# VectorE's outer products of batch 0 in one place, the key-value sums ahead of the denominators, q's second half turned between them; block 10's w_out product whole

## The chip, the cores and the metric

The kernel runs on one core of a Trainium2 chip. The metric is the device time of one execution in microseconds (us). Five engines matter here: TensorE (PE in the profile, its weight loads PEld), VectorE (DVE), ScalarE (ACT), GpSimd (POOL), and SyncE (SP), whose queue issues nearly all of the DMAs. Each engine works through its own instructions in order and waits on semaphores for the others.

## The reference

Two stages, the first feeding the second:

```python
# q, k, v: (4 batches, 4 heads, 1088 tokens, 32); S1, S2: (8, 32)
phi(x)  = outer(S1 x, S2 x)                      # 64 features a token
kv, z   = sum_s phi(k)_s v_s, sum_s phi(k)_s      # per batch and head
attn    = (phi(q) kv) / (phi(q) z + 1e-6)
x       = attn as (4352 tokens, 128)
out     = (sigmoid(x @ w_gate) * (x @ w_val)) @ w_out    # d_ff 1536
```

S1, S2 and the three weights arrive as 64-bit floats, and the kernel makes 32-bit floats of them itself.

## The kernel before

**The steady part.** The tokens are cut into nine chunks `ci` (eight of 512, one of 256). For each chunk and each of the twelve blocks j of 128 columns of d_ff, one *wave* (`w1`, L541) multiplies the chunk's attention result `xT` by block j of w_gate and of w_val into a PSUM tile `wave`; ScalarE makes the sigmoid `sg` (L564), VectorE the product `g` (L599), and TensorE multiplies `g` by block j of w_out. `slot` (L625) writes the order out by hand: in each slot the `g` of the wave before, the w_out products that have fallen due (list `todo`), then the next wave. Chunk 0 uses `w2` (L418), due two waves later; later chunks use an arrangement with fewer multiplications (`w2_a`, `w2_b`, L381), and the last one `w2_end`. In chunk 0 the waves use the whole array (128x128 weights); from chunk 1 on each wave is cut into two halves of 64 columns of the array that run side by side. In `w2`, blocks 0 to 9 are whole (`d = slice(0, P)`, L424), blocks 10 and 11 in two such halves. Block 10's product stands behind chunk 0's last wave and ahead of `kps(1)`, the first product of batch 1.

The attention work of batches 1 to 3 is put between waves (`plan`, L1353). Batch 0's can't be: no wave can start before its first 256 tokens are in `xT`. So the kernel has a *head*, the code from L1147 to L1249, which is what the change touches most.

**The head.** In the order in which the program issues it:

1. q, k, v and the weights are loaded (L282 to L293). SP's DMAs, in order: S, q's first half (8 of 17 pairs of rows), block 0 of w_gate and w_val, v, block 1 of both, w_out's first two blocks (`load_w_out(0)`, L289), q's second half (L290), then the other weights.
2. VectorE turns k and q's first half (`turn_k`, `turn_q(0, 0)`). `kps` (L683) gives S k for all tokens, `ab` (L784) S q for the first 512 tokens.
3. `gram` (L710) gives the sums z from products of S k with itself; GpSimd masks them (`gh`, L727), `spread_z` (L738, a matmul) spreads them, `mask_z` (L747, VectorE) makes the weights `zb` of the denominators.
4. `outer` (L769) forms phi(k) for nine blocks of tokens, `kp`. For each pair of heads pi, GpSimd does blocks 6 to 8 (L1206), VectorE blocks 0 to 4 (L1211) and, later, block 5 (L1220).
5. `mult00` and `mult10` (L819, VectorE) form phi(q), `qp`.
6. `kv0` (L894) multiplies v by phi(k): `kvz` in bank acc1, a matmul for each block and head. Each head has a strip of 32 columns of the array. Blocks 0 to 4 come before `mult00`, blocks 5 to 8 inside `rest`.
7. `dn(0, 0, rest)` (L1077): the denominators `dps` (L1083), then `rest` (L1218): block 5's outer products, the last `kv0`, the denominators turned (`dT`, L1094), 1e-6 added by ScalarE (`rc`), `kvz` copied (`kvd`, L934), steps of the weights, `ndt` (L959: kv turned, `ndps` and its copy `nd`); then the numerators `nps` (L1102).
8. `divide` (L1112): reciprocal, `rb` (the reciprocals spread, L1131), `between`, and the product `xT` (L1121), each for 256 tokens. `between` is `head1` (L1233): q's second half turned (`turn_q(0, 1)`), steps of the weights, and `qcomp` (L830: `cqps`, its ScalarE copy `cq`) with the DMAs that spread it.
9. `slot(None, 1)`: the first wave, whose first half needs 256 tokens of `xT` and block 0 of w_gate and w_val.

**Weights on the way.** `Short` (L129) makes 32-bit numbers in steps that go from engine to engine: `bounds` (ACT `cap`, then POOL `head` L141), `lower` (`tail`, ACT or DVE), `shift` (DVE L157), `total` (POOL L162), `sign` (ACT L168), `final` (DVE L171 into `w_sb`). Piece 0 is block 0 of w_gate and w_val, piece 1 block 1, piece 2 the first two blocks of w_out, piece 3 block 2 of all three, and so on.

Of the kernel before, what the change touches and what calls it, by code (L numbers as in the profile page):

```python
# [16 lines left out]
P = 128  # L17
# [3 lines left out]
def kernel(  # L21
# [12 lines left out]
    nc = tc.nc  # L34

    B, H, S, D = q.shape
# [4 lines left out]
    NJ = DFF // P  # L41
    assert DM == H * D == P and D == 32 and R == 8 and S % 32 == 0 and NTOK % 512 == 256

    T = S // 32

    NJK = 9
# [14 lines left out]
    psm = ctx.enter_context(tc.tile_pool(name="psm", bufs=2, space=bass.MemoryType.PSUM))  # L61
# [14 lines left out]
    T0 = 2 * q_chk[0][1]  # L76
# [116 lines left out]
    def load_w_in(j0, j1):  # L193
        cs = slice(j0 * P, j1 * P)
        n, jj = divmod(j0, 2)
        if wide and jj == 0:
            w_in[n] = raw.tile([P, 3, 2, P, 2], I32, tag="w_in", name="w_in")
        for i, src in enumerate((moe_w_gate, moe_w_val)):
            if wide:
                nc.sync.dma_start(  # L200
                    out=w_in[n][:, i, jj : jj + j1 - j0].rearrange("p j m w -> p (j m w)"),
                    in_=src[:, cs].bitcast(I32),
                )
            else:
                nc.sync.dma_start(
                    out=w_sb[:, i, j0:j1].rearrange("p j m -> p (j m)"), in_=src[:, cs]
                )

    def load_w_out(n):
        j0, j1 = 2 * n, 2 * n + 2  # L210
        cs = slice(j0 * P, j1 * P)
        src = moe_w_out[cs, :].bitcast(I32) if wide else moe_w_out[cs, :]
        nc.sync.dma_start(
            out=w_in[n][:, 2].rearrange("p j m w -> p j (m w)") if wide else w_sb[:, 2, j0:j1],
            in_=src.rearrange("(j p) m -> p j m", p=P),
        )
# [3 lines left out]
    def step(name, *parts, **how):  # L220
        for n in parts if wide else ():
            if n not in short:

                i = ((slice(0, 2), 0), (slice(0, 2), 1), (2, slice(0, 2)))[n] if n < 3 else (slice(0, 3), n - 1)
                pair, jj = (0, i[1]) if n < 3 else divmod(n - 1, 2)
                short[n] = Short(w_sb[:, i[0], i[1]], w_in[pair][:, i[0], jj])
            getattr(short[n], name)(**how)
# [15 lines left out]
    def load_rows(src, b, t, parts=((0, T, nc.sync),)):  # L243
        for t0, t1, eng in parts:
            eng.dma_start(
                out=t[:, t0:t1, :],
                in_=bass.AP(
                    tensor=src.tensor,
                    offset=src[b, 0].offset + t0 * D,
                    ap=[[T * D, P], [1, (t1 - t0) * D]],  # L250
                ),
            )

    v_sb = ld.tile([P, H, NJK, D], F32, tag="v", name="v")
    def load_v(b):
        base = v[b, 0].offset
        for g in range(4):
            j = g // 2
            nc.sync.dma_start(
                out=v_sb[32 * g : 32 * g + 32, :, j:],  # L260
                in_=bass.AP(
                    tensor=v.tensor,
                    offset=base + (KBASE[g] + j) * D,
                    ap=[[T * D, 32], [S * D, H], [1, (NJK - j) * D]],
                ),
            )

    k_t, q_t = {}, {}
# [17 lines left out]
    load_w_in(0, 1)  # L286
    load_v(0)
    load_w_in(1, 2)
    load_w_out(0)  # L289
    load_rows(q, 0, q_t[0], ((T0, T, nc.sync),))  # L290
    for n in range(1, NJ // 2):
        load_w_in(2 * n, 2 * n + 2)
        load_w_out(n)  # L293
# [124 lines left out]
    def w2(ci, j0, jn, g):  # L418
        if j0 == 0:
            moe["sum"] = ci  # L420
            moe["acc"] = pso.tile([P, TCH], F32, tag="acc0", name="moeout")
        for jj in range(jn):
            j = j0 + jj
            for d in (slice(0, P),) if j < NJ - 2 else (slice(0, 64), slice(64, P)):  # L424
                nc.tensor.matmul(  # L425
                    out=moe["acc"][d],
                    lhsT=w_sb[:, 2, j, d],
                    rhs=g[:, jj],
                    start=(j == 0),
                    stop=(j == NJ - 1),  # L430
                )
        if j0 + jn == NJ:
            o_sb = sbA.tile([P, TCH // 32, 32], F32, tag="o_sb", name="o_sb")
            nc.vector.transpose(out=o_sb.rearrange("p t d -> p (t d)"), in_=moe["acc"])
            moe["store"] = lambda: store(
                ci, lambda g4: o_sb[32 * g4 : 32 * g4 + 32], nc.scalar
            )
# [229 lines left out]
    def turn_q(b, n):  # L667
        if b >= B:
            return
        if n == 0:  # L670
            qT_of[b] = sbA.tile([P, TP, 2, 32], F32, tag="qT", name="qT", bufs=1)
        t0, tn = q_chk[n]
        nc.vector.transpose(
            out=qT_of[b][:, t0 : t0 + tn].rearrange("p t c s -> p (t c s)"),
            in_=q_t[b][:, 2 * t0 : 2 * (t0 + tn)].rearrange("p t d -> p (t d)"),
        )
# [92 lines left out]
    def outer(b, pi, j0=0, j1=NJK, eng=nc.vector):  # L769
        a0 = KAB[b][:, pi, j0:j1]  # L770
        ap = [list(a0.ap[0]), [2 * R, 2 * (j1 - j0)]]
        eng.tensor_tensor(  # L772
            out=KP[b][:, pi, j0:j1].rearrange("p j m (i l) -> p (j m) i l", i=R),
            in0=bass.AP(tensor=a0.tensor, offset=a0.offset, ap=ap + [[1, R], [0, R]]),
            in1=bass.AP(tensor=a0.tensor, offset=a0.offset + R, ap=ap + [[0, R], [1, R]]),
            op=MUL,
        )
# [113 lines left out]
        q0 = half(QP[b], n)  # L891
        nc.vector.tensor_tensor(out=q0, in0=q0, in1=half(BQ[b], n), op=MUL)  # L892

    def kv0(j_list):  # L894
        if 0 not in KVZ:
            KVZ[0] = pso.tile([P, TCH], F32, tag="acc1", name="kvz")
        for j in j_list:
            for h in range(H):
                nc.tensor.matmul(
                    out=KVZ[0][32 * h : 32 * h + 32, :F],  # L900
                    lhsT=v_sb[:, h, j, :],
                    rhs=KP[0][:, h // 2, j, h % 2, :],
                    start=(j == 1),
                    stop=(j == NJK - 1),
                    skip_group_check=True,
                )
# [23 lines left out]
    def kvd(b):  # L930
        KVD[b] = sbA.tile([P, 2, 2, F], F32, tag="kvd", name="kvd")
        k0 = KVZ[b][:, : 2 * F]
        n = 2 if b > 0 else 1
        nc.scalar.copy(  # L934
            out=KVD[b][:, :n],
            in_=bass.AP(
                tensor=k0.tensor, offset=k0.offset, ap=[list(k0.ap[0]), [F, n], [0, 2], [1, F]]
            ),
        )
# [19 lines left out]
    def ndt(b):  # L959
        if b == 0:  # L960
            t = pso.tile([P, TCH], F32, tag="acc1", name="ndps")
            ndps = t.rearrange("p (w x) -> p w x", w=2)
        else:
            ndps = ps2.tile([P, 2, 512], F32, tag="two", name="ndps")[:, 0].rearrange(
                "p (w x) -> p w x", w=2
            )
        if b == 0:
            nc.tensor.matmul(
                out=ndps[:, 0, :P],
                lhsT=KVD[b][:, 0].rearrange("p c f -> p (c f)"),  # L970
                rhs=ident,
                is_transpose=True,
                start=True,
                stop=True,
            )
        for c in range(2 if b else 0):
            nc.tensor.matmul(
                out=ndps[64 * c : 64 * c + 64, 0, :P],
                lhsT=KVD[b][:, 0, c],
                rhs=ident,  # L980
                start=True,
                stop=True,
            )
        ND[b] = sbA.tile([P, P], F32, tag="nd", name="nd")
        nc.scalar.copy(out=ND[b], in_=ndps[:, 0, :P])
# [222 lines left out]
    step("lower", 0, 1)  # L1208
    spread_z()
    for pi in range(2):  # L1210
        outer(0, pi, 0, 5)  # L1211
    kv0([1, 2, 3, 4, 0])
    mult00()
    mult10()
    mask_z()


    def rest(turn, rc, dT):  # L1218
        for pi in range(2):
            outer(0, pi, 5, NJK - 3)  # L1220
        kv0(range(5, NJK))
        turn()
        nt = rc.shape[1] - 1
        nc.scalar.activation(out=rc[:, :nt], in_=dT[:, :nt, :2], func=ACTF.Identity, bias=eps)
        kvd(0)
        step("shift", 0, 1)
        step("total", 0, 1)
        step("sign", 0, bank="acc0")
        ndt(0)

    divide = dn(0, 0, rest)

    def head1():  # L1233
        turn_q(0, 1)
        step("final", 0)
        step("sign", 1, bank="acc1")
        step("bounds", 2)
        step("lower", 2)
        step("bounds", 3)
        spread(0, (1,), qcomp(0, (1,), (psm, "wave")), nc.sync, nc.sync)  # L1240

    divide((0, 4), (4, 8), between=head1)
    step("final", 1)
    step("shift", 2, 3)
# [169 lines left out]
```

## Time and profile before

| | us |
|---|---|
| median of three runs | 290.53 (290.02 to 291.15) |
| the profiled execution | 289.88 |
| its span in the profile | 288.1 |
| TensorE busy | 282.3 (98%) |
| VectorE, GpSimd, ScalarE busy | 171.2, 159.7, 106.7 |
| first wave's first matmul | 14.44 |
| last matmul of the program issued | 284.6 |

Times in the profile count from the start of the span. What lies around the span in the profiled execution is 289.88 - 288.1 = 1.8 us. A line of the timeline gives the start, the length and the engine, then the line of the program, the operation, what it writes and reads, and how many instructions are put together in the line; for an x2 line the length is from the first one's start to the last one's end. VectorE's and ScalarE's instructions are pipelined, so that the next one often starts up to 0.1 us before the end of the one before. A 32-bit matmul stands as two instructions. The granted TensorE clock is at its full 1.0 in all slices.

### The profile page before, as it was taken

To read this page: it belongs to the slowest core of one execution; us is meant where nothing else is said; L and a number is where in the kernel's file an instruction comes from. 1 tells how busy PE (TensorE), PEld (TensorE's weight loads), DVE (VectorE), ACT (ScalarE), POOL (GpSimd) and SP (SyncE) were. 2 spreads that over 40 slices of the span, in tenths; PEclk is the share of its full clock that TensorE was granted. 3 is DMA by queue.
4 is the path that set the end of the run, shared out by engine and by line. 5 is a ranking of instruction groups with operands and counts; after the bars stand their busy time and mean duration, and the time that the engine had idled before them with its cause. 6 is when DMAs were issued, how large, how long until landed. Compare 5 with 4: busy or idle time off the path is not lost.

```text
span 288.1 us, 5789 instructions
## 1 busy us (share of the span) xinstructions
PE 282.3 (98%) x2262; PEld 134.4 (47%) x2262; DVE 171.2 (59%) x294; ACT 106.7 (37%) x215; POOL 159.7 (55%) x222
## 2 busy tenths in 40 slices
PE   8799999999999999999999999999999999999995
PEld 3454433354444444535444445444444444444685
DVE  6987788946748547668446485767245223522571
ACT  3788832222334322523244222532243224421341
POOL 2666682667466387383565496483564646555200
PEclk9999999999999999999999999999999999999999
DMA  7995441765700386451000673020001000020012
GB/s 215 338 371 122 111 156 43 167 143 126 207 2 2 77 192 155 108 164 29 1 0 12 159 181 102 2 30 9 0 3 23 14 2 0 4 35 1 0 19 40
DMA packets 28891, 24.24 MB, mean 84 GB/s; under 512 B 18560, under 2 KB 24064, under 8 KB 28864
## 3 DMA queue, kind: packets, MB, share of 16 engines
q1 hardware_dynamic: 25888, 22.10, 29.8%
q10 hardware_dynamic: 2976, 1.77, 2.1%
q8 instruction: 18, 0.29, 0.5%
q14 instruction: 9, 0.07, 0.1%
HBM read 20.60 MB, written 3.26 MB: 83 GB/s over the span
## 4 chain that ended last, share of the span: by engine, by line
PE 97%; ACT 1%; DVE 1%; issue 0%; POOL 0%
PE wave L556 61%; PE prod L381 22%; PE moeout L425 4%; PE moeout L451 2%; PE warm L301 2%; PE kvz L912 1%; PE nps L1271 1%; PE kps L693 1%; PE cqps L839 1%; PE nps L1102 0%; PE denj L1041 0%; PE dps L1083 0%; PE nps L1054 0%; ACT asb L810 0%; DVE qp L819 0%; PE aps L800 0%
## 5 line engine op out<-in xcount | busy, mean ns | idle before, releaser
L556 PE MATMUL wave<-xT,w_sb 128*64 128x512 f32 (+3 forms) x820 | 201.4, 565 | 0.0
L564 ACT ACTIVATE sg<-wave 128x512 f32<-128x512 f32 x102 | 60.9, 597 | 158.0 <-PE wave L556 152.0
L599 DVE TENSOR_TENSOR g<-wave,sg 128x512 f32<-128x512 f32 x96 | 66.0, 688 | 87.6 <-ACT sg L564 86.1
L371 POOL TENSOR_TENSOR tsum<-g,tsum 128x256 f32<-128x256 f32 x84 | 67.5, 804 | 71.0 <-DVE g L599 70.8
L556 PEld LDWEIGHTS wave<-xT,w_sb 128*64 128x64 f32 (+1 forms) x820 | 71.0, 140 | 72.5 <-issue 53.0
L371 POOL TENSOR_TENSOR tsum<-g 128x256 f32<-128x256 f32 x84 | 67.5, 804 | 22.3 <-DVE g L599 21.7
L381 PE MATMUL prod<-tsum,ws 128*64 128x256 f32 x252 | 68.4, 380 | 0.0
L381 PE MATMUL prod<-g,w_sb 128*64 128x256 f32 (+1 forms) x170 | 50.3, 378 | 0.0
L381 PEld LDWEIGHTS prod<-tsum,ws 128*64 128x64 f32 x252 | 34.0, 137 | 13.1 <-issue 9.7
L381 PEld LDWEIGHTS prod<-g,w_sb 128*64 128x64 f32 x170 | 23.0, 137 | 30.1 <-issue 25.8
L381 PE MATMUL prod<-tsum,w_sb 128*64 128x256 f32 x84 | 25.0, 380 | 0.0
L381 PE MATMUL prod<-g,ws 128*64 128x256 f32 x84 | 25.0, 379 | 0.0
L162 POOL TENSOR_TENSOR head<-head,tail 128x384 int32<-128x384 int32 (+1 forms) x13 | 13.2, 1022 | 4.3 <-DVE head L157 4.3
L381 PEld LDWEIGHTS prod<-g,ws 128*64 128x64 f32 x84 | 11.5, 137 | 5.7
L425 PE MATMUL moeout<-g,w_sb 128*128 128x512 f32 (+1 forms) x28 | 12.4, 600 | 0.0
L381 PEld LDWEIGHTS prod<-tsum,w_sb 128*64 128x64 f32 x84 | 11.3, 137 | 1.3 <-issue 1.0
L892 DVE TENSOR_TENSOR qp<-qp,bq 128x1152 f32<-128x1152 f32 (+1 forms) x7 | 10.5, 1502 | 0.3 <-DMA bq<-dq 0.3
L772 DVE TENSOR_TENSOR kp<-kab 128x1152 f32<-128x1152 f32 (+2 forms) x10 | 10.7, 1081 | 0.0
L592 DVE TENSOR_TENSOR g<-wave,sg 128x512 f32<-128x512 f32 x6 | 6.8, 1132 | 6.3 <-ACT sg L564 4.7
L496 DVE TENSOR_TENSOR res<-prod,other 128x256 f32<-128x256 f32 x14 | 5.9, 425 | 6.3 <-ACT other L487 4.8
L141 POOL TENSOR_SCALAR head<-cap 128x384 f32<-128x384 f32 (+1 forms) x13 | 6.3, 487 | 5.2 <-ACT cap L140 5.2
L152 ACT ACTIVATE tail<-w_in,two__157 128x384 f32<-128x384 uint32 (+1 forms) x12 | 7.2, 610 | 0.0
(130 smaller groups left out, 196.0 us busy)
## 6 DMA issues: line engine op xcount, KB each, us to landing
qp<-dq SPq DMA_DIRECT2D x7, 576.0 KB
bq<-dq SPq DMA_DIRECT2D x14, 288.0 KB
kq<-in_k_dram SPq DMA_DIRECT2D x3, 544.0 KB
kq<-in_q_dram SPq DMA_DIRECT2D x3, 544.0 KB
w_in<-in_moe_w_out_dram SPq DMA_DIRECT2D x6, 256.0 KB
w_in<-in_moe_w_gate_dram SPq DMA_DIRECT2D x5, 256.0 KB
w_in<-in_moe_w_val_dram SPq DMA_DIRECT2D x5, 256.0 KB
v<-in_v_dram SPq DMA_DIRECT2D x8, 144.0 KB
```

What stands on the lines that cost most here:

```text
L141: nc.gpsimd.tensor_scalar(out=self.head.bitcast(F32), in0=self.cap, scalar1=122880.0, scalar2=2.0**-15, op0=ALU.min, op1=ALU.max,)
L152: nc.scalar.activation(out=self.tail, in_=self.lo, func=ACTF.Identity, bias=two, scale=2.0**-51)
L162: nc.gpsimd.tensor_tensor(out=self.head, in0=self.head, in1=self.tail.bitcast(I32), op=ALU.add)
L371: nc.gpsimd.tensor_tensor(out=t[:, u], in0=in0, in1=in1, op=ALU.subtract)
L381: nc.tensor.matmul(out=out, lhsT=lhsT, rhs=rhs, start=start, stop=stop, skip_group_check=True)
L425: nc.tensor.matmul(out=moe["acc"][d], lhsT=w_sb[:, 2, j, d], rhs=g[:, jj], start=(j == 0), stop=(j == NJ - 1),)
L556: nc.tensor.matmul(out=wv[d, which, jj * tw + o : jj * tw + o + tp], lhsT=w_sb[:, which, j0 + jj, d], rhs=xT[:, t0 + o : t0 + o + tp], sta ...
L564: nc.scalar.activation(out=sg, in_=wv[:, 0], func=ACTF.Sigmoid)
L592: nc.vector.tensor_tensor(out=g.rearrange("p (j u s y) -> p j y u s", j=2, u=2, y=4), in0=wv[:, 1].rearrange("p (j y u s) -> p j y u s", j ...
L599: nc.vector.tensor_tensor(out=g, in0=wv[:, 1], in1=sg, op=MUL)
L772: eng.tensor_tensor(out=KP[b][:, pi, j0:j1].rearrange("p j m (i l) -> p (j m) i l", i=R), in0=bass.AP(tensor=a0.tensor, offset=a0.offset, ...
L892: nc.vector.tensor_tensor(out=q0, in0=q0, in1=half(BQ[b], n), op=MUL)
```

## The change

Five edits, all in the head but the second:

- q's second half is loaded ahead of w_out's first blocks.
- Block 10's w_out product of chunk 0 is whole; only block 11 stays in halves.
- VectorE's outer products cover blocks 0 to 5 in one instruction for each pair of heads. All of `kv0` stands ahead of `mult00` and of the denominators: blocks 1 to 5 and 0 for all heads, then GpSimd's blocks 6 to 8 for heads 0 and 1, then for heads 2 and 3.
- `turn_q(0, 1)` and `kvd(0)` come ahead of `dn`, and `ndt(0)` is the first thing in `rest`. So VectorE has q's second half between `zb` and `dT`, and ScalarE copies `kvd` and `nd` before `rc`.
- In `head1`, `spread` with `qcomp` comes ahead of `step("bounds", 3)`.

```diff
     load_w_in(1, 2)
+    load_rows(q, 0, q_t[0], ((T0, T, nc.sync),))
     load_w_out(0)
-    load_rows(q, 0, q_t[0], ((T0, T, nc.sync),))
...
-            for d in (slice(0, P),) if j < NJ - 2 else (slice(0, 64), slice(64, P)):
+            for d in (slice(0, P),) if j < NJ - 1 else (slice(0, 64), slice(64, P)):
...
-    def kv0(j_list):
+    def kv0(j_list, heads=range(H)):
...
         for j in j_list:
-            for h in range(H):
+            for h in heads:
...
     for pi in range(2):
-        outer(0, pi, 0, 5)
-    kv0([1, 2, 3, 4, 0])
+        outer(0, pi, 0, NJK - 3)
+    kv0([1, 2, 3, 4, 5, 0])
+    for pi in range(2):
+        kv0(range(NJK - 3, NJK), (2 * pi, 2 * pi + 1))
     mult00()
     mult10()
     mask_z()
+    turn_q(0, 1)
+    kvd(0)
 
 
     def rest(turn, rc, dT):
-        for pi in range(2):
-            outer(0, pi, 5, NJK - 3)
-        kv0(range(5, NJK))
+        ndt(0)
         turn()
         nt = rc.shape[1] - 1
         nc.scalar.activation(out=rc[:, :nt], in_=dT[:, :nt, :2], func=ACTF.Identity, bias=eps)
-        kvd(0)
         step("shift", 0, 1)
         step("total", 0, 1)
         step("sign", 0, bank="acc0")
-        ndt(0)
 
     divide = dn(0, 0, rest)
 
     def head1():
-        turn_q(0, 1)
         step("final", 0)
         step("sign", 1, bank="acc1")
         step("bounds", 2)
         step("lower", 2)
+        spread(0, (1,), qcomp(0, (1,), (psm, "wave")), nc.sync, nc.sync)
         step("bounds", 3)
-        spread(0, (1,), qcomp(0, (1,), (psm, "wave")), nc.sync, nc.sync)
```

## The prediction

> **What bounds the kernel.** I read first the share of busy time (TensorE 98%), then what TensorE itself waited for, over the whole program:
>
> ```profile
> PE dps L1083 <- DVE zb L762: 0.5, 1, 0.5
> PE ndps L968 <- ACT kvd L934: 0.5, 1, 0.5
> PE nps L1102 <- ACT nd L985: 0.4, 1, 0.4
> PE gram L739 <- POOL gh L727: 0.3, 1, 0.3
> ```
>
> Beside 0.8 us at the very start, that is all, and all of it lies in the head. From the first wave at 14.44 us on, TensorE has no idle time that the profile shows. So a change can pay in two ways only: an earlier first wave, or fewer TensorE microseconds behind it. The timelines by engine give the head, VectorE first:
>
> ```profile
> 7.49 1.52 DVE L772 TENSOR_TENSOR kp<-kab 128x640 f32<-128x640 f32 x2
> 8.99 1.29 DVE L819 TENSOR_TENSOR qp<-bps,asb 128x512 f32<-128x512 f32 x2
> ...
> 10.58 0.68 DVE L772 TENSOR_TENSOR kp<-kab 128x128 f32<-128x128 f32 x2
> 11.51 0.45 DVE L1094 STREAM_TRANSPOSE dT<-dps 128x256 f32<-128x256 f32 x1 [0.24 <-PE dps L1083]
> ...
> 12.62 0.45 DVE L1131 STREAM_TRANSPOSE rb<-rc 128x256 f32<-128x256 f32 x1
> 12.99 0.74 DVE L673 STREAM_TRANSPOSE qT<-kq 128x576 f32<-128x576 f32 x1
> 13.65 0.39 DVE L171 TENSOR_TENSOR w_sb<-square,head 128x256 f32<-128x256 f32 x1
> 13.96 0.42 DVE L1121 TENSOR_TENSOR xT<-nps,rb 128x256 f32<-128x256 f32 x1
> ```
>
> From `dT` to `xT` VectorE never waits 0.15 us; q's second half (`qT`) stands in the middle of that chain, and the product `xT` (done at 14.38) releases the first wave. GpSimd's and TensorE's lines:
>
> ```profile
> 8.65 0.46 POOL L727 TENSOR_TENSOR gh<-gs,e_m 128x32 f32<-128x32 f32 x1 [2.37 <-ACT gs L725]
> 9.07 1.65 POOL L772 TENSOR_TENSOR kp<-kab 128x384 f32<-128x384 f32 x2
> ```
>
> ```profile
> 9.50 0.77 PE L899 MATMUL kvz<-kp,v 128*32 128x64 f32 x40
> 10.81 0.64 PE L1083 MATMUL dps<-qp,zb 128*32 128x256 f32 x8 [0.55 <-DVE zb L762]
> ...
> 42.63 1.02 PE L425 MATMUL moeout<-g,w_sb 128*128 128x512 f32 x2
> 43.49 1.88 PE L556 MATMUL wave<-xT,w_sb 128*128 128x512 f32 x4
> 45.30 1.08 PE L425 MATMUL moeout<-g,w_sb 128*64 128x512 f32 x4
> 46.31 0.72 PE L693 MATMUL kps<-kT,sk 64*32 64x288 f32 x16
> ```
>
> The reader is to see that GpSimd's outer products run from 9.07 to 10.72, and that `dps` starts at 10.81, 0.14 behind `zb` (10.45 to 10.67).
>
> **Outer products in one place.** VectorE: the 640-element instruction takes 0.78 (7.49 to 8.27, the next starts at 8.19), the 128-element one 0.28. The slope is 0.50 / 512, so 768 elements cost 0.125 more each, 0.25 for two. The two small ones (0.68 behind `zb`) go. So `mult00` starts at 9.24, `zb` ends at 10.92.
>
> What else is late by that? `gh` is a small GpSimd instruction (128x32), yet it takes 0.46; a GpSimd copy of the same 128x32 at 6.05 takes 0.23. It ends at 9.11, 0.10 behind VectorE's second outer product (8.19 to 9.01). So I take it to be held by that one. The latter now ends at 9.26, `gh` at 9.36, and GpSimd's two outer products, right behind it, at 10.97 and not 10.72. The bounds for `gh`: not held at all, 0.00 later; held, 0.25 later. I take 0.25, by its own row. The Trainium skill weighs on the same side: "SBUF — State Buffer", section "Who interferes with whom", says that a VectorE instruction with two SBUF inputs and a GpSimd instruction that reads SBUF exclude each other for a whole instruction. That speaks against this change, which lengthens such an instruction just where GpSimd is waiting: by the rule the head's gain is the 0.05 below, without it the 0.32 of the first rival. The row alone leaves both readings open; the trace has no `gh` without a neighbour.
>
> **kv ahead of the denominators.** TensorE works in order, so `dps` now also waits for all of `kvz`, and the last twelve of its instructions (blocks 6 to 8 of heads 2 and 3) wait for GpSimd's second outer product: 10.97, plus 0.05 to the first matmul (VectorE's small product ended at 11.27, the weight load behind it came at 11.32). They use two strips of columns, six on each. The 40 at 9.50 use four strips, ten on each, and start within 0.77 - 0.22 (the last one's length) = 0.55, so 0.056 a step. Six steps: 0.34. `dps` starts at 11.36 instead of 10.81: +0.55. (By `zb` alone it would be 11.07.) Bounds of a step: 0.056, and 0.11, a weight load's length, if nothing overlaps on a strip. I take the first, which is measured.
>
> `kvd` and `ndt` come off the path: `kvz` is done at 11.57, `kvd` at 11.9, `ndps` behind `dps` at 12.3, `nd` at 12.6, the numerators end at 13.3 instead of 13.86. That gain has no taker: `xT` waits for `rb` and its place on VectorE.
>
> **q's second half moved.** On VectorE it stands between `zb` and `dT`: 10.84 to 11.58, while `dT` can't start before 12.06 (11.51 + 0.55). Free, with 0.48 to spare. Its data must be there by 10.84. SP has eight DMAs under way, and the one issued at 11.07 was released by q's second half, the one at 10.30 by w_out's first blocks (SP's waits name them). Exchanged, q lands near 10.3 and w_out near 11.05; the latter is first used at 13.5. On SP's queue nothing else changes place but these two (0.44 and 0.45 to issue). `qcomp`'s matmuls now end at 13.9 instead of 14.47.
>
> From `dT` on: before, `dT` 11.51, `rb` 12.62, `qT`, weights 13.65, `xT` 13.96. After: `dT` 12.06, `rb` 13.17, then the weights of block 0 at once (13.54) if GpSimd's `total` is there. `shift` starts 0.37 behind `dT`, `total` 0.40 behind that and lasts 0.73 (12.28 to 13.01 before): 13.56, plus 0.04. So weights 13.60, `xT` +0.31 = 13.91, first wave at 14.39: 0.05 earlier. In sum, 0.66 of `qT` and wait gone, 0.55 later `dps`, 0.06 of wait for GpSimd.
>
> Behind it the first wave's second matmul stood 0.32 behind the first instead of the later 0.22, beside `cqps`, which ended at 14.47; that 0.10 goes as well. But the first w_out product waits for VectorE's `g`, before at 17.15 to 17.83 with the product at 17.99. Its predecessors (`cap` of block 2, now behind the copy `cq` on ScalarE, GpSimd's `head` and `total`, the weights) come out within 0.05 of where they were, so I count 0.05 and not 0.15. Head: **-0.05**.
>
> **Block 10 whole.** A whole product costs 0.86 (42.63 to 43.49), a wave between whole products 1.72 (40.91 to 42.63). Where the shape of the weights changes, time is added: this wave takes 1.81 (43.49 to 45.30), the two halves 1.01 (45.30 to 46.31). After: wave 1.72, whole product with the change of shape behind it 0.86 + 0.09 = 0.95; 2.82 becomes 2.67, **-0.15**. Bounds: 0 if the array needs more between 128x128 and the 64x32 of `kps` (the switch from whole to 128x32 at 38.68 shows 0.09 too), -0.19 if that costs nothing.
>
> **Sum.** -0.05 - 0.15 = -0.20: the profiled 289.88 would be 289.68. That execution is 0.65 below the median of the three runs, so I apply the difference to the median: 290.53 - 0.20 = **290.3**. All this is far inside 0.5% (1.45 us), about what a measurement of this kernel can tell from no change.
>
> **Rivals.**
>
> - *`gh` isn't held.* GpSimd is done at 10.72, the last `kvz` at 11.1, `dps` at `zb` + 0.14 = 11.07 or just behind, +0.26 instead of +0.55. Weights at 13.31, first wave at 14.11: -0.32, with block 10 -0.47, **290.05**. For it: the extra length of `gh` could be its odd access pattern. Against: the 0.10 behind VectorE's end.
> - *Slower: `dps` queued behind a slow pair of strips.* If six matmuls on a strip take 0.11 each and not 0.056, the last `kvz` starts at 11.68 and `dps` is 0.87 late. The first wave then comes at 14.71, +0.27 (+0.32 on what I forecast), with block 10 **290.65**. It decides from the point where `dps` starts later than 11.56 (0.20 more than forecast eats the whole gain). With no overlap at all, a matmul's 0.22 a step, 1.0 more than forecast: 291.3. Against it: every `kvz` row has the quick pace, though on four strips. A late q transfer would act at the same place, but only from 11.36 on, 1.0 behind where I expect it.
> - *Block 10's saving doesn't come:* the time of the change of shape reappears ahead of `kps`. Head alone: **290.5**.
>
> **The numbers.** Forecast 0.50, `gh` not held 0.22, slow strips 0.19, no saving 0.09. The forecast's own spread is the runs' (290.02 to 291.15 for one kernel, about 0.6 either way). The range goes from 0.45 below the first rival to 0.55 above the second, most of that spread: 289.6 to 291.2. Faster by over 0.5% (below 289.08) needs the first rival with more than it can explain: 0.03. Slower by over 0.5% (above 291.98) needs the strips at their worst and something behind them: 0.06. Within: 0.91.
>
> **What would show it.** `gh` ending 0.1 behind VectorE's second outer product, near 9.36; GpSimd's outer products ending near 10.97; a stretch of idle TensorE before the last twelve `kvz`; `dps` near 11.36 and no longer released by `zb`; `qT` without a wait from 10.84; `xT` near 13.91, first wave near 14.39; at 45 us a wave of 1.72 and a product of 0.95. I am wrong if `dps` still follows `zb`, if `qT` waits for its DMA, or if TensorE waits anywhere behind the first wave.

## The result, and the profile after

The change makes the kernel slower by a little: 290.63 us (median of 22 runs) against 289.96 for the kernel before in the same comparison, a ratio of 1.0026 with a 95% interval of 1.0016 to 1.0037. Two more comparisons of the same kernel gave 1.0007 (0.9998 to 1.0016) and 1.0011 (0.9992 to 1.0029). All three are within 0.5%. The forecast was 0.20 us faster, so the sign was wrong. The 290.3 itself was reckoned from 290.53, the median of three runs, while longer series of the kernel before have medians of 289.96 to 290.19.

The profiled execution has a span of 289.0 us (288.1 before). First, what TensorE waited for in the whole program, of the kernel after (`PEq` is TensorE's own sequencer; the three numbers are the us in total, the times, and the longest):

```profile
PE warm L301 <- PEq L1397: 0.8, 1, 0.8
PE wave L556 <- DVE xT L1121: 0.6, 1, 0.6
PE gram L739 <- POOL gh L727: 0.5, 1, 0.5
PE nps L1102 <- ACT nd L985: 0.4, 1, 0.4
PE moeout L425 <- DVE g L599: 0.3, 1, 0.3
```

Two lines are new. The `wave` line lies ahead of the first wave, as forecast: what stands before `xT` on TensorE is done sooner, and nothing takes the gain. The last line is the one that the prediction named as a sign of being wrong: TensorE waits *behind* the first wave, for the first `g`. TensorE's timeline of the kernel after (start, length, line, operation):

```profile
10.29 1.63 PE L899 MATMUL kvz<-kp,v 128*32 128x64 f32 x66
11.74 0.41 PE L1083 MATMUL dps<-qp,zb 128*32 128x256 f32 x2
11.75 0.34 PE L899 MATMUL kvz<-kp,v 128*32 128x64 f32 x6
11.92 0.60 PE L1083 MATMUL dps<-qp,zb 128*32 128x256 f32 x6
...
14.92 3.71 PE L556 MATMUL wave<-xT,w_sb 128*128 128x256 f32 x12 [0.63 <-DVE xT L1121]
18.95 1.13 PE L425 MATMUL moeout<-g,w_sb 128*128 128x512 f32 x2 [0.32 <-DVE g L599]
...
44.55 1.88 PE L556 MATMUL wave<-xT,w_sb 128*128 128x512 f32 x4
46.27 1.02 PE L425 MATMUL moeout<-g,w_sb 128*128 128x512 f32 x2
47.22 0.71 PE L693 MATMUL kps<-kT,sk 64*32 64x288 f32 x16
```

VectorE's, GpSimd's and ScalarE's, same kernel:

```profile
8.01 1.79 DVE L772 TENSOR_TENSOR kp<-kab 128x768 f32<-128x768 f32 x2
...
11.30 0.77 DVE L673 STREAM_TRANSPOSE qT<-kq 128x576 f32<-128x576 f32 x1
12.57 0.45 DVE L1094 STREAM_TRANSPOSE dT<-dps 128x256 f32<-128x256 f32 x1 [0.50 <-PE dps L1083]
...
14.45 0.41 DVE L1121 TENSOR_TENSOR xT<-nps,rb 128x256 f32<-128x256 f32 x1
...
15.92 0.28 DVE L157 TENSOR_SCALAR head<-head 128x256 int32<-128x256 int32 x1
16.63 0.87 DVE L157 TENSOR_SCALAR head<-head 128x384 int32<-128x384 int32 x1 [0.43 <-POOL head L141]
17.43 0.54 DVE L148 TENSOR_SCALAR tail<-w_in 128x384 f32<-128x384 uint32 x1
17.89 0.41 DVE L171 TENSOR_TENSOR w_sb<-square,head 128x256 f32<-128x256 f32 x1
18.22 0.67 DVE L599 TENSOR_TENSOR g<-wave,sg 128x512 f32<-128x512 f32 x1
```

```profile
9.15 0.75 POOL L727 TENSOR_TENSOR gh<-gs,e_m 128x32 f32<-128x32 f32 x1 [2.75 <-ACT gs L725]
9.86 1.65 POOL L772 TENSOR_TENSOR kp<-kab 128x384 f32<-128x384 f32 x2
...
16.09 0.51 POOL L141 TENSOR_SCALAR head<-cap 128x384 f32<-128x384 f32 x1 [0.96 <-ACT cap L140]
16.56 0.72 POOL L162 TENSOR_TENSOR head<-head,tail 128x256 int32<-128x256 int32 x1
```

```profile
14.79 0.63 ACT L847 COPY cq<-cqps 64x576 f32<-64x576 f32 x1
15.45 0.56 ACT L140 ACTIVATE cap<-w_in 128x384 f32<-128x384 f32 x1
```

**How to compare two such profiles.** VectorE's outer products start at 8.01 here and at 7.49 before, though nothing of the change is ahead of them. So a plain comparison of start times mixes this offset with the change. I cut the span at four instructions instead: the start of VectorE's first outer product, the first wave's first matmul, the first w_out product (`moeout`), and `kps` of batch 1. This is the table for all kernels of the study (us; each cell is a difference of two start times, the last piece ends with the span):

| kernel | outer products start | to first wave | to first w_out product | to `kps` of batch 1 | to the end | sum from outer products |
|---|---|---|---|---|---|---|
| before | 7.49 | 6.95 | 3.55 | 28.32 | 241.79 | 280.61 |
| after | 8.01 | 6.91 | 4.03 | 28.27 | 241.79 | 280.99 |
| after_again | 7.56 | 6.91 | 4.04 | 28.27 | 241.79 | 281.01 |
| after_third | 7.75 | 6.91 | 4.02 | 28.27 | 241.79 | 280.99 |
| a_bounds_first | 7.50 | 6.91 | 3.55 | 28.17 | 241.79 | 280.42 |
| b_spread_first | 8.10 | 6.95 | 4.27 | 28.42 | 241.79 | 281.42 |
| b_whole | 7.91 | 6.95 | 3.55 | 28.17 | 241.80 | 280.47 |
| pool_pause | 7.63 | 6.90 | 3.77 | 28.27 | 241.79 | 280.73 |
| a_split | 7.51 | 6.82 | 4.04 | 28.27 | 241.78 | 280.91 |
| kv_behind | 7.60 | 6.80 | 3.55 | 28.17 | 241.91 | 280.43 |
| mixed | 7.83 | 6.80 | 3.55 | 28.17 | 241.79 | 280.31 |
| seven | 7.61 | 6.83 | 3.55 | 28.17 | 241.79 | 280.33 |
| turn_back | 7.56 | 7.47 | 3.55 | 28.17 | 241.79 | 280.98 |
| q_behind | 7.57 | 6.91 | 3.55 | 28.17 | 241.79 | 280.41 |

Everything behind 47 us is the same to 0.01 in nearly all of them (`kv_behind` has 0.12 more, all of it behind the program's last matmul); the three profiles of the changed kernel agree within 0.02 in every piece. So single profiles can be read to a few hundredths here, once cut this way. The change in profile terms: first wave 0.04 earlier, first w_out product 0.48 later against that wave, 0.05 back by `kps` of batch 1. Sum: **+0.39 us**, a ratio of 1.0013.

### The profile page after: what moved, and what is told of

Same layout as the page of the kernel before. It is cut to its first block, busy times and chain, and to the rows that moved or that the text cites. A ratio compares the mean times of both kernels' runs of the same rounds, so it can differ in the third digit from the quotient of the medians.

```text
span 289.0 us, 5783 instructions
## 1 busy us (share of the span) xinstructions
PE 283.0 (98%) x2260; PEld 134.9 (47%) x2260; DVE 170.7 (59%) x292; ACT 106.8 (37%) x215; POOL 159.7 (55%) x222
## 4 chain that ended last, share of the span: by engine, by line
PE 95%; ACT 1%; POOL 1%; issue 1%; DVE 1%; DVEq 0%
PE wave L556 60%; PE prod L381 22%; PE moeout L425 4%; PE moeout L451 2%; PE warm L301 2%; PE kvz L912 1%; PE nps L1270 1%; PE kps L693 1%; POOL kp L772 1%; PE cqps L839 1%; PE denj L1041 0%; PE nps L1054 0%; PE dps L1083 0%; ACT asb L810 0%; ACT cap L140 0%
## 5 line engine op out<-in xcount | busy, mean ns | idle before, releaser
L371 POOL TENSOR_TENSOR tsum<-g,tsum 128x256 f32<-128x256 f32 x84 | 68.4, 815 | 71.1 <-DVE g L599 71.0
L371 POOL TENSOR_TENSOR tsum<-g 128x256 f32<-128x256 f32 x84 | 66.4, 791 | 22.2 <-DVE g L599 21.6
L772 DVE TENSOR_TENSOR kp<-kab 128x1152 f32<-128x1152 f32 (+1 forms) x8 | 10.2, 1288 | 0.0
L425 PEld LDWEIGHTS moeout<-g,w_sb 128*128 128x128 f32 (+1 forms) x26 | 4.3, 181 | 6.5 <-issue 3.4
```

Source lines behind the costliest of these rows:

```text
L371: nc.gpsimd.tensor_tensor(out=t[:, u], in0=in0, in1=in1, op=ALU.subtract)
L425: nc.tensor.matmul(out=moe["acc"][d], lhsT=w_sb[:, 2, j, d], rhs=g[:, jj], start=(j == 0), stop=(j == NJ - 1),)
L772: eng.tensor_tensor(out=KP[b][:, pi, j0:j1].rearrange("p j m (i l) -> p (j m) i l", i=R), in0=bass.AP(tensor=a0.tensor, offset=a0.offset, ...
```

## The experiments

My theory after this result (A): the wait for `g` is the loss, and it comes from the smallest edit, `spread` ahead of `step("bounds", 3)`. ScalarE makes the copy `cq` (14.79) first, `cap` of piece 3 comes late (15.45), and with it GpSimd's `head`, and VectorE's `shift` of piece 3. The rival (B): `g` is late because `kv` ahead of the denominators pushes VectorE's whole chain.

### One edit taken out, one edit alone

`a_bounds_first`, on the changed kernel:

```diff
+        step("bounds", 3)
         spread(0, (1,), qcomp(0, (1,), (psm, "wave")), nc.sync, nc.sync)
-        step("bounds", 3)
```

> The changed kernel with one line put back: in head1 step("bounds", 3) is again ahead of spread. Theory A: in the changed kernel ScalarE makes the copy cq before cap of piece 3, so GpSimd's head of piece 3, its total of piece 2 and VectorE's shift of piece 3 fall in another order, VectorE's first g is late and the first w_out product waits (0.32 in the changed kernel's profile, 4.03 from the first wave's first matmul to the first w_out product instead of 3.55). Then this run has that distance back near 3.55, no wait of TensorE for g, and is 0.4 to 0.5 us faster than the changed kernel: ratio to before near 1.0010 instead of 1.0026. Rival B: g is late because kv ahead of the denominators pushes all of VectorE's chain; then the distance stays at 4.03 and the ratio at 1.0026.

`b_spread_first`, the opposite swap in `head1` of the kernel before, with nothing else changed.

> The kernel before with only spread put ahead of step("bounds", 3) in head1. Theory A: cap of piece 3 starts behind cq, at 15.1 or later instead of 14.63, the first g is late and the first w_out product waits for it: 0.3 to 0.5 us slower than before, ratio 1.0010 to 1.0017. Rival B: no difference from before, ratio 1.0000.

TensorE's and VectorE's timeline in `a_bounds_first`:

```profile
14.42 3.71 PE L556 MATMUL wave<-xT,w_sb 128*128 128x256 f32 x12 [0.63 <-DVE xT L1121]
17.96 1.02 PE L425 MATMUL moeout<-g,w_sb 128*128 128x512 f32 x2
```

```profile
15.42 0.55 DVE L157 TENSOR_SCALAR head<-head 128x256 int32<-128x256 int32 x2
15.89 0.55 DVE L148 TENSOR_SCALAR tail<-w_in 128x384 f32<-128x384 uint32 x1
16.59 0.42 DVE L171 TENSOR_TENSOR w_sb<-square,head 128x256 f32<-128x256 f32 x1 [0.16 <-POOL head L162]
```

And TensorE in `b_spread_first`:

```profile
15.05 3.71 PE L556 MATMUL wave<-xT,w_sb 128*128 128x256 f32 x12
19.32 1.13 PE L425 MATMUL moeout<-g,w_sb 128*128 128x512 f32 x2 [0.56 <-DVE g L599]
```

With the edit taken out the distance is 3.55 and there is no wait; with the edit alone it is 4.27 with a wait of 0.56. The times agree: 1.0004 (0.9994 to 1.0014) without the edit, 1.0035 (1.0017 to 1.0052) with the edit alone. That is more than I expected (1.0010 to 1.0017), and so is the profile: 281.42 against 280.61, 0.81 or 1.0028. There `cq` also waits for q's second half turned late and ends 7.68 behind the start of the outer products (7.41 in the changed kernel), and `cap` is behind it. Theory A holds and B falls. Without that one swap the profile is 280.42, 0.19 *below* the kernel before: the forecast's -0.20. The interval of the time can't show so little.

### Why a late `cap` costs so much

`cap` of piece 3 is only 0.33 later against `xT` (14.63 - 13.96 = 0.67 before, 15.45 - 14.45 = 1.00 after), but `g` is 0.58 later (3.19 and 3.77). In the kernel before, ScalarE, VectorE (`shift` of piece 3, the weights of w_out, `g`), GpSimd (`total` of piece 2) and TensorE stand so:

```profile
14.63 0.55 ACT L140 ACTIVATE cap<-w_in 128x384 f32<-128x384 f32 x1 [0.26 <-issue]
```

```profile
15.84 0.34 DVE L157 TENSOR_SCALAR head<-head 128x384 int32<-128x384 int32 x1
...
16.81 0.42 DVE L171 TENSOR_TENSOR w_sb<-square,head 128x256 f32<-128x256 f32 x1 [0.16 <-POOL head L162]
17.15 0.68 DVE L599 TENSOR_TENSOR g<-wave,sg 128x512 f32<-128x512 f32 x1
```

```profile
16.00 0.77 POOL L162 TENSOR_TENSOR head<-head,tail 128x256 int32<-128x256 int32 x1 [0.23 <-DVE head L157]
```

```profile
17.99 1.02 PE L425 MATMUL moeout<-g,w_sb 128*128 128x512 f32 x2
```

Here the first w_out product starts 0.16 behind the end of `g` (17.83), right behind the wave's last matmul; in the kernel after it starts 0.06 behind the end of `g` (18.89). So `g` had 0.10 to spare, and its 0.58 are 0.48 at the product.

In the kernel after, `total` comes first (16.56, its `shift` long done), and `shift` of piece 3 starts 0.07 later and takes 0.87 instead of 0.34. It ends (17.50) 0.22 behind the end of `total` (17.28). In `b_spread_first` and `a_split` it also ends 0.22 and 0.21 behind. So it looks held by GpSimd's instruction. `lower` and the weights of w_out queue behind it on VectorE, and `g` behind them. To test this I gave GpSimd something else to do first. `pool_pause`, on the changed kernel:

```diff
         step("bounds", 3)
+        nc.gpsimd.memset(pause, 0.0)
 
+    pause = const.tile([P, 128], F32, tag="pause", name="pause")
     divide((0, 4), (4, 8), between=head1)
```

> The changed kernel with one GpSimd instruction more: a memset of 128x128 (0.2 us) right behind head of piece 3, that is between it and total of piece 2. Theory: in the changed kernel total starts 0.07 ahead of VectorE's shift of piece 3 and holds it (shift 0.87 long instead of 0.35), which makes g late. With GpSimd kept away for 0.2 us, shift starts first and is 0.35 long, total starts 0.2 later and ends 0.2 to 0.25 later, the weights of w_out 0.3 earlier; the first w_out product stands about 3.7 behind the first wave instead of 4.03, so that an added instruction makes the kernel 0.3 us faster. Rival: the shift isn't held, g is late because cap of piece 3 is; then the added instruction makes it no better, 4.03 or more.

GpSimd, VectorE and TensorE in `pool_pause`:

```profile
15.70 0.51 POOL L141 TENSOR_SCALAR head<-cap 128x384 f32<-128x384 f32 x1 [0.96 <-ACT cap L140]
16.15 0.20 POOL L1240 MEMSET pause<- 128x128 f32 x1
16.32 1.84 POOL L162 TENSOR_TENSOR head<-head,tail 128x256 int32<-128x256 int32 x2
```

```profile
16.24 0.36 DVE L157 TENSOR_SCALAR head<-head 128x384 int32<-128x384 int32 x1 [0.42 <-POOL head L141]
```

```profile
14.53 3.71 PE L556 MATMUL wave<-xT,w_sb 128*128 128x256 f32 x12 [0.63 <-DVE xT L1121]
18.30 1.13 PE L425 MATMUL moeout<-g,w_sb 128*128 128x512 f32 x2
```

One useless instruction more, and the first w_out product comes 0.26 sooner behind the wave (3.77 instead of 4.03); `shift` is 0.36 long. The time, 1.0008 (0.9999 to 1.0017), fits and can't decide by itself. So the hold is shown, and whichever of the two starts first holds the other.

The run gives back 0.26 of the 0.48 and not all of it, because the memset puts `total` off and `shift` now holds `total`: it takes 0.87, ends at 17.19, and the weights of w_out follow at 17.22. What the hold costs without a memset can only be reckoned. In the times of the kernel before, and with its lengths, `total` would run from 16.04 to 16.76, and the weights would start near 16.84 (`shift` at 16.11, `lower` 0.27 behind it, the weights 0.46 behind that), 0.03 later than the 16.81 of before, so that the product would not wait. By this estimate the hold is all of the 0.48; a run shows 0.26 of it.

### Block 10 alone

`b_whole` is the kernel before with `NJ - 2` changed to `NJ - 1` in `w2`, nothing else.

> The kernel before with only block 10's w_out product whole. As predicted: at 43 us a wave of 1.72 and a product of 0.95 where 1.81 and 1.01 stood, 0.15 us faster, ratio 0.9995. Rival: the time of the change of shape reappears in kps, ratio 1.0000.

From the first w_out product to `kps` of batch 1 it needs 28.17 instead of 28.32: -0.15 as forecast, with a wave of 1.72 and a product of 0.95. The time, 0.9999 (0.9988 to 1.0010), can't resolve it. In the changed kernel the piece is 28.27: after the wait for `g` the second matmul of that first product stands 0.53 behind the first instead of 0.43, which takes 0.10 of it back.

### Is `gh` held by VectorE's outer product?

`a_split`, on the changed kernel:

```diff
     for pi in range(2):
-        outer(0, pi, 0, NJK - 3)
+        for j0, j1 in ((0, 6),) if pi == 0 else ((0, 3), (3, 6)):
+            outer(0, pi, j0, j1)
```

> The changed kernel with VectorE's outer product of the second pair of heads cut in two (blocks 0 to 2, 3 to 5). If gh is held by one VectorE instruction at a time, it now ends 0.1 behind the first of the two, 0.4 earlier against that chain; GpSimd's outer products and the last kvz follow, dps is again near zb + 0.14, and the first wave comes 0.2 to 0.3 earlier: ratio near 1.0017. If gh's length is its own, it ended 0.75 behind its start anyhow and nothing moves but VectorE's 0.06 for the extra instruction: ratio 1.0028. Third possibility: the second half takes its inputs before gh gets a turn, and gh is held by both: no gain either, but gh still ends 0.1 behind the last.

GpSimd in `a_split`:

```profile
8.68 0.32 POOL L727 TENSOR_TENSOR gh<-gs,e_m 128x32 f32<-128x32 f32 x1 [2.37 <-ACT gs L725]
8.96 1.96 POOL L772 TENSOR_TENSOR kp<-kab 128x384 f32<-128x384 f32 x2
```

`gh` is 0.32 long instead of 0.75 and ends at 8.99, 0.09 behind the first of the two halves (8.35 to 8.90). So it is held by one VectorE instruction at a time. But the next GpSimd instruction then meets the other half (8.81 to 9.41) and takes 1.15 instead of 0.84, so that the two outer products take 1.96 instead of 1.65. The first wave gains 0.09 only, not the 0.2 to 0.3 I expected; the time is 1.0017 (1.0003 to 1.0031), where 1.0017 was expected, with an interval too wide for a verdict between 0.1 and 0.3.

`seven` moves block 6 from GpSimd to VectorE, on `a_bounds_first`:

```diff
-        outer(0, pi, NJK - 3, NJK, eng=nc.gpsimd)
+        outer(0, pi, NJK - 2, NJK, eng=nc.gpsimd)
...
-        outer(0, pi, 0, NJK - 3)
-    kv0([1, 2, 3, 4, 5, 0])
+        outer(0, pi, 0, NJK - 2)
+    kv0([1, 2, 3, 4, 5, 6, 0])
     for pi in range(2):
-        kv0(range(NJK - 3, NJK), (2 * pi, 2 * pi + 1))
+        kv0(range(NJK - 2, NJK), (2 * pi, 2 * pi + 1))
```

> a_bounds_first with block 6 moved from GpSimd's outer products to VectorE's (seven and two). By the chain GpSimd outer products, last kvz, dps: zb 0.25 later, gh 0.25 later (held by the longer instruction), GpSimd's outer products end 0.27 earlier, last dps instruction 4.02 behind the start instead of 4.14, the first wave 0.1 earlier. If a longer VectorE instruction costs more than GpSimd's shorter ones give back, the wave is 0.25 later.

The last `dps` stands 4.05 behind the start (4.02 expected, 4.13 in `a_bounds_first`), the first wave at 6.83, 0.08 earlier. `gh` is now 0.98 long, held by the longer product to its end. Time: 1.0010 (0.9991 to 1.0030), no verdict.

### The denominators behind kv, and q's second half

`kv_behind`, on `a_bounds_first`:

```diff
-    for pi in range(2):
-        kv0(range(NJK - 3, NJK), (2 * pi, 2 * pi + 1))
...
     turn_q(0, 1)
-    kvd(0)
...
     def rest(turn, rc, dT):
-        ndt(0)
+        kv0(range(NJK - 3, NJK))
+        kvd(0)
         turn()
...
         step("sign", 0, bank="acc0")
+        ndt(0)
```

> a_bounds_first with the matmuls of blocks 6 to 8 (kv0), kvd and ndt put back behind the denominators; VectorE's six blocks and q's second half stay where the change put them. Theory: what makes dps late in the changed kernel is the wait for GpSimd's outer products ahead of it (dps 0.55 later than before, of which zb explains 0.26). Then the first dps stands 0.14 behind zb again, 3.51 behind the start of the outer products and its last instruction 3.77 (4.14 in a_bounds_first); xT is then held by nps instead, at 6.25, the first wave at 6.73 instead of 6.92: 0.19 us faster than a_bounds_first, ratio to before 0.9990 to 0.9998. Rival: kvz, kvd, ndps, nd in a row behind dps cost as much as they do in the kernel before, and the wave stays at 6.9 or later.

TensorE in `kv_behind`:

```profile
11.12 0.64 PE L1083 MATMUL dps<-qp,zb 128*32 128x256 f32 x8 [0.36 <-DVE zb L762]
11.55 0.54 PE L899 MATMUL kvz<-kp,v 128*32 128x64 f32 x24
```

`dps` is released by `zb` again and stands at 3.51 (last one 3.77), just as expected. `xT` comes at 6.33 and not 6.25, the first wave at 6.80 and not 6.73: the row `kvz`, `kvd`, `ndps`, `nd`, `nps` was 0.07 longer than I reckoned. Gain over `a_bounds_first` in the head: 0.11. Time: 0.9994 (0.9985 to 1.0003).

`mixed` puts only heads 2 and 3 of those blocks behind the denominators:

```diff
     kv0([1, 2, 3, 4, 5, 0])
+    kv0(range(NJK - 3, NJK), (0, 1))
...
-        kv0(range(NJK - 3, NJK))
+        kv0(range(NJK - 3, NJK), (2, 3))
```

> kv_behind with blocks 6 to 8 of heads 0 and 1 ahead of the denominators and those of heads 2 and 3 behind. By the theory dps needs zb alone (3.51 behind the start of the outer products) and only twelve matmuls stand between dps and kvd, so nps and with it xT come 0.17 earlier than in kv_behind: xT near 6.16, first wave near 6.64, span's end near 280.15 counted from that start; ratio to before 0.9980 to 0.9990. If dps still waits for GpSimd, or something else than nps holds xT in kv_behind, it stays at 6.80.

No gain: 6.80 again, against 6.64 expected. Twelve `kvz` on two strips take 0.51 where 24 on four took 0.54. What counts is six steps on a strip, not how many matmuls there are. I had used that rule in the prediction and forgot it here. Time: 0.9993 (0.9985 to 1.0002). `kv_behind` and `mixed` have the lowest ratios of the study; each one's interval still reaches 1.0.

`turn_back` moves `turn_q(0, 1)` back to the top of `head1`, on `a_bounds_first`.

> a_bounds_first with q's second half turned in head1 again, between rb and the weights of block 0. Theory: the 0.66 of that place is what pays for the later dps; put back, xT and the first wave come 0.6 later (7.5 behind the start of the outer products instead of 6.92), ratio to before 1.002 to 1.003. Rival: VectorE's place is not what holds xT (GpSimd's total or nps does), and the wave moves by under 0.2.

The first wave comes at 7.47 (7.5 expected): q's place on VectorE was worth 0.56. By its profile the kernel would be 0.37 slower than before, 1.0013; it measured 1.0044 (1.0028 to 1.0060) from four runs. Much of the excess lies outside the profiled span: the four spans have a median of 288.65, 0.35 above the 288.30 of the kernel before in the same comparison, but 1.83 to 2.85 lie around them, against 1.74 to 1.94 there. Why that is so stays open.

`q_behind` gives `a_bounds_first` the load order of the kernel before.

> a_bounds_first with q's second half loaded behind w_out's first blocks, as in the kernel before. By the estimate q then lands near 11.05, so that turning it waits some 0.2 us, but dT comes only at 12.06 and nothing else moves: first wave at 6.91 behind the start of the outer products. A rival that gives the load order a price sees the wave later.

In the one execution of it, the wave stands at 6.91, and VectorE's only wait of 0.15 or more from 9 to 15 us is `dT`'s for `dps`. So this edit was free either way.

### The time of the changed kernel

> The changed kernel unaltered, for a second profile. Its first profile starts VectorE's outer products at 8.01, the kernel before's at 7.49, with nothing of the change ahead of them; the clock that TensorE was granted stepped up at 6.7 and 5.5. If that is chance of the execution, this profile may start anywhere from 7.5 to 8.1, and counted from there the first wave stands at 6.9, the first w_out product 4.0 behind it and the span's end at 281.0, as in the first. If it belongs to the changed kernel, the start is near 8.0 again.

> The changed kernel unaltered a third time, for its time. The first comparison gave 1.0026 (1.0016 to 1.0037), the second 1.0007 (0.9998 to 1.0016). By the profiles the change costs 0.39 us, a ratio of 1.0013, once the chance start of the head is taken off. If that is all, this interval holds 1.0013; if the changed kernel has a cost that the profiles miss, the ratio is near 1.0026 again.

The second profile starts its outer products at 7.56, the third at 7.75, so the 8.01 of the first is chance. In all profiles the start goes with the moment at which the record of TensorE's granted clock begins: 3.7 to 5.5 us with starts of 7.49 to 7.63, from 6.1 to 7.0 with 7.75 to 8.10 (between them, 5.73 with 7.91 and 5.74 with 7.56). Up to that moment TensorE goes at half its later pace, which the slices of the page don't show: the warm-up's 256-column matmuls stand 0.43 apart ahead of it (4.31 and 4.74 in the kernel before) and 0.22 apart behind it (4.03 and 4.25 in `kv_behind`, where it comes at 3.74). The second and third intervals hold the 1.0013 that the profiles give. The first (from 1.0016) is just above it; the spans of its runs have a median of 288.8, against 288.6 and 288.5 of the changed kernel in the later two. I take that for the spread of the start, but no run shows why it fell so.

## Why the prediction was wrong, point by point

All times of the changed kernel less 0.52, the offset of the start (8.01 - 7.49).

- *Outer products and `gh`.* Forecast: `gh` to 9.36, GpSimd's outer products to 10.97. Measured: 9.37 and 10.98. (`zb` ended at 10.86, 0.06 sooner than forecast, off the path.) `gh` ended 0.09 to 0.10 behind the VectorE instruction beside it in all fourteen profiles, with lengths from 0.32 to 0.98. The Trainium skill, "SBUF — State Buffer", section "Who interferes with whom", says that a VectorE instruction with two SBUF inputs contends with a GpSimd instruction that reads SBUF, under an exclusive lock; these rows agree.
- *kv ahead of the denominators.* Forecast +0.55 for `dps`. The last one came at 11.62, +0.55; `dT` at 12.05, +0.54. In one thing the trace differs: the first two `dps` went ahead of the last six `kvz`, though the program has them behind. So "TensorE works in order" is not strictly so here; the last `dps` came as forecast all the same.
- *q's second half.* No wait, from 10.78 on; 0.50 idle behind it. Right, and worth 0.56 by `turn_back`.
- *First wave.* Forecast 14.39, measured 14.40: 0.04 earlier than before, forecast 0.05.
- *The step that failed:* "Its predecessors (...) come out within 0.05 of where they were, so I count 0.05 and not 0.15." The first w_out product was forecast near 17.94 and came at 18.43. The weights of w_out's first blocks came at 17.37 and not within 0.05 of 16.81. I had put `cq` ahead of `cap`, but let each later instruction keep its length of before. I counted the hold between VectorE and GpSimd at `gh`, where I was looking, and not at `shift` and `total`, where the same edit exchanged who is first. `shift` took 0.87 and not 0.34; the first w_out product came 0.48 later against the wave (0.26 of it shown to be the hold by `pool_pause`, the rest reckoned), and its second matmul another 0.10 behind the wait. The same passage has the product wait for `g` in the kernel before; there it stood right behind the wave's last matmul, with 0.10 to spare. The 0.10 that I saw in the first wave's second matmul as a neighbour's doing is there without the neighbour (14.92 after 0.63 of idle time, the next 0.32 behind): it was never to be had.
- *Block 10.* -0.15 forecast; -0.15 in `b_whole`. (By the figures beside it, the bound for a change of shape that costs nothing is 2.82 - 1.72 - 0.86 = 0.24, not 0.19.) In the changed kernel 0.10 of it is taken back by the wait.
- *Sum.* -0.04 + 0.48 + 0.10 - 0.15 = +0.39 instead of -0.20. The other terms held to 0.03 (`dT` to `xT` is 0.57 shorter, forecast 0.60); `a_bounds_first`, which lacks only the failed step, is at -0.19.
- *Rivals.* `gh` not held: no. Slow strips: the sign came true, the mechanism did not (0.056 a step on two strips too). That its 290.65 lies beside the measured 290.63 is luck. No saving by block 10: no.

## What to carry to other kernels

When a step moves, ask for each instruction behind it not only when its inputs are ready, but also which instruction of another engine that can hold it will now start first; here 0.07 us decided whether `shift` took 0.36 or 0.87. A term worked out from old lengths is only good as long as the pairs of instructions that overlap stay the same. To compare two profiles to a few hundredths, cut them at the same instructions and compare the pieces, so that the chance of the start drops out.

## What the runs showed of the hardware

- VectorE's `shift` (`TENSOR_SCALAR`, 384 int32 numbers) and GpSimd's `total` (`TENSOR_TENSOR`) hold each other. `shift` took 0.34 to 0.36 when it started ahead of `total`, and 0.87 to 0.88 when it started 0.06 to 0.07 behind it, ending 0.21 to 0.22 behind its end in five profiles. `total` took 0.72 to 0.73 when it was first, and 0.77 to 0.78 (eight profiles) or 0.87 (`pool_pause`) when it was second, ending 0.58 to 0.59 behind the end of `shift` in nine profiles.
- From these rows: the one that starts second ends behind the first by its own length less about 0.14 (0.72 - 0.58 for `total`, 0.36 - 0.22 for `shift`, 0.84 - 0.70 for GpSimd's outer product in `a_split`, which ended at 10.11 against 9.41). So the hold is full both ways but for the first 0.14 of the instruction that is held. That is an estimate from these pairs.
- TensorE takes a matmul ahead of others that the program has in front of it: two `dps` at 11.74, ahead of the last six `kvz` of heads 2 and 3.
- After a wait of 0.32, a product of two 512-column matmuls has 0.53 between its starts instead of 0.43.
